# Attention scores with the key's low part against the query's high part alone, in half-height products

## The chip, the cores and the metric

The kernel runs on one core of one Trainium2 chip. The core's engines work side by side and each takes its own instructions in order: TensorE (PE in the profile; its weight loads are shown as PEld), VectorE (DVE), ScalarE (ACT), GpSimd (POOL), and SyncE (SP), which issues the transfers. The metric is the device time of one execution in microseconds.

## The reference

A block of three parts: attention with a bias that a small network makes of the distance of two positions, then a feed-forward layer with a ReLU6 gate, then one with a sigmoid gate.

```python
# attention: batch 4, heads 8, seq 576, head_dim 64
scores = scale * np.matmul(q, k.transpose(0, 1, 3, 2))
x = (psi_rel / psi_i)[..., None]
h = np.maximum(x @ w1 + b1, 0.0)
bias = h @ w2
scores = scores + bias.transpose(2, 0, 1)[None, :, :, :]
scores = scores - np.max(scores, axis=-1, keepdims=True)
attn = np.exp(scores)
attn = attn / (np.sum(attn, axis=-1, keepdims=True) + 1e-09)
y = np.matmul(attn, v)
# 2304 tokens of width 512; d_ff 2048, then 1536
h = x @ w_in;  z = (h * np.clip(h + 3.0, 0.0, 6.0) / 6.0) @ w_out
gate = 1.0 / (1.0 + np.exp(-(z @ w_gate)));  out = (gate * (z @ w_val)) @ w_out2
```

## The kernel before, in words

**Stages.** First the bias is computed and written to DRAM (products of L490). Then comes attention, and then the two feed-forward layers, whose products stand at L511 to L513, L575 and L632. The change touches attention alone, and the two calls of `prep` for the first unit, which stand in the bias stage.

**Units, steps and slots.** The 32 pairs of batch and head are taken two heads at a time: 16 units n, each with nine steps s. Steps 0 to 7 are one head h = s % 2 and one block of 128 queries c = s // 2. Step 8 has the last 64 queries of both heads. `slot_of_two` takes two steps at a time, so two units fill nine slots; in one of the nine the two steps are step 8 of a unit and step 0 of the next, and in another they are steps 7 and 8. A slot issues the scores of its own steps, then the products with the values (`av`) of older steps, then the exponentials, then the transposes of the probabilities of the slot before (`trans`, `trans_rem`), and last the preparation of a coming unit (`prep`). The framework's scheduler then orders each engine's instructions; the order that results is shown below.

**Scores.** Queries and keys are split in two parts of type fp32r: a high part, which is the rounded value, and a low part, the rest. The stationary operand `Q` has 128 rows: the 64 of the high part and, below them, the 64 of the low part. `K` holds the key's high part twice, one copy above the other, and the low part likewise, since the keys are loaded into both halves of the partitions. So one product of 128 rows with K's high part, and one with its low part, make a full product of both. With two halves of 288 keys (a = 0, 1) that is four products of 128 rows and 288 columns for a step, and eight for step 8 (L262). VectorE then adds the bias and takes the row's extreme in one instruction (L266); ScalarE exponentiates (L282).

**Around them.** The probabilities are transposed on TensorE: `tr` at L320, L335, L338 and L339 with 128 rows, L299 for the inverse sums, and L328 for step 8, in which a stationary operand has 64 rows, four products on the upper 64 rows of the array and four on the lower. `av` (L352) multiplies in fp32 with a stationary operand of 64 columns, one head on each half of the columns; L355 is its remainder with 128 columns. One `av` product leaves two records in the trace.

**Preparation.** `prep` makes the parts of one head: the query's high part on ScalarE (L230), the key's high part (L234), the query's low part and the key's low part (L238) on GpSimd. For unit 0 ScalarE and VectorE do it.

Of the kernel before, what the change touches and what calls it, by code (L numbers as in the profile page):

```python
# [10 lines left out]
F32 = mybir.dt.float32  # L11
F32R = mybir.dt.float32r
I32 = mybir.dt.int32
AF = mybir.ActivationFunctionType
ALU = mybir.AluOpType
# [3 lines left out]
P = 128  # L19
B, H, S, D = 4, 8, 576, 64  # L20
# [4 lines left out]
HS = S // 2  # L25
# [6 lines left out]
QH = (slice(0, S + 64), slice(S + 64, QW))  # L32
# [63 lines left out]
def block_kernel(ctx: ExitStack, tc: tile.TileContext, q, k, v, mlp, w_in, w_out, w_gate, w_val, w_out2, dist_d,  # L96
                 rows_d, out):
    nc = tc.nc
# [7 lines left out]
    one = keep.tile([P, 1], F32, name="one")  # L106
# [78 lines left out]
    apool = attn.enter_context(tc.tile_pool(name="apool", bufs=1))  # L185
    a2 = attn.enter_context(tc.tile_pool(name="a2", bufs=2))
# [3 lines left out]
    qn, kn, vn = {}, {}, {}  # L190
    cut = np.cumsum([0, QW, 2 * S, S // 2, 35, NPSI])
    q_in, k_in, bpsi, mlpc, rows = [early[:, i:j] for i, j in zip(cut, cut[1:])]
# [1 line left out]
    bias_t = [apool.tile([P, 2, S], F32, name=f"bias{c}") for c in range(4)]  # L194
    bias_m = apool.tile([P, S], F32, name="bias_m")
    Qs = [apool.tile([P, QW], F32R, name=f"q{i}") for i in range(2)]
    Ks = [apool.tile([P, 2, 2, S], F32R, name=f"k{i}") for i in range(2)]
    Pm = [apool.tile([P, S + 64], F32, name=f"pm{i}") for i in range(2)]
    ident = apool.tile([P, P], F32, name="ident")
    stat = apool.tile([P, 5, NSTEP], F32, name="stat")  # L200
# [4 lines left out]
    corr = apool.tile([P, 2], F32, name="corr")  # L205

    def load_qk(n):
        qn[n], kn[n] = q_in[0:D], k_in
        nc.sync.dma_start(qn[n], q[n])
        for r in range(2):  # L210
            nc.sync.dma_start(kn[n][D * r : D * r + D], k[n])

# [10 lines left out]

    def prep(n, h, on=PREP_ON):

        Q, K, qt, kt = Qs[n % 2][:, QH[h]], Ks[n % 2][:, :, h], qn[n][:, QH[h]], kn[n][:, h]

        def high(eng, out, x):
            if eng == "A":
                nc.scalar.copy(out, x)  # L230
            elif eng == "V":
                nc.vector.tensor_copy(out, x)
            else:
                nc.gpsimd.tensor_tensor(out=out, in0=x, in1=one[0 : x.shape[0]].to_broadcast(x.shape), op=ALU.mult)  # L234

        def low(eng, out, x, hi):
            eng = nc.vector if eng == "V" else nc.gpsimd
            eng.tensor_tensor(out=out, in0=x, in1=hi.bitcast(F32), op=ALU.subtract)  # L238

        high(on[0], Q[0:D], qt)  # L240
        high(on[1], K[:, 0], kt)
        low(on[2], Q[D:P], qt, Q[0:D])
        low(on[3], K[:, 1], kt, K[:, 0])

    halves = lambda ap: ap.rearrange("p (a b) -> p a b", a=2)
    NS = NU * NSTEP
# [3 lines left out]

    seq = [(n, s) for n in range(NU) for s in range(NSTEP)]

    def scores(t):
        n, s = seq[t]
        Q, K = Qs[n % 2], Ks[n % 2]
        ps = pp.tile([P, 2, 512], F32, name="s")
        todo = [(s % 2, s // 2)] if s < 8 else [(0, 4), (1, 4)]
        for a in range(2):
            mm = [(h, c, r) for h, c in todo for r in range(2)]
            for i, (h, c, r) in enumerate(mm):  # L260
                q0 = (0, S + P)[h] + P * c if c < 4 else (512, S)[h]
                last_s[0] = nc.tensor.matmul(ps[:, a, 0:HS], Q[:, q0 : q0 + P], K[:, r, h, HS * a : HS * a + HS],  # L262
                                 start=(i == 0), stop=(i == len(mm) - 1))
        u = a2.tile([P, S], F32, name="u", bufs=3)
        bt = bias_t[s // 2][:, s % 2] if s < 8 else bias_m
        last_u[0] = nc.vector.tensor_tensor_reduce(  # L266
            out=halves(u), in0=ps[:, :, 0:HS], in1=halves(bt), op0=ALU.add, op1=ALU.min, scale=-0.125, scalar=3e38,
            accum_out=low[n % 2][:, s : s + 1])
        us[t] = u

    def probs(t):
        n, s = seq[t]
# [94 lines left out]
    for n in range(NU):  # L367
        i = (NSTEP * n + 5) // 2 + 2
# [5 lines left out]
    def steps(i):  # L374
        return [t for t in (2 * i, 2 * i + 1) if 0 <= t < NS]

    def slot_of_two(i):

        for t in steps(i):
            scores(t)  # L380
            n, s = seq[t]
            p, b = divmod(n, B)
            if s == 0:
                last_v[0] = load_v(n)
            if b == B - 1 and p + 1 < NPAIR and (s % 2 == 1 or s == 8):
                load_bias(p + 1, s // 2)
        for n, a, g in AV.get(i, ()):
            av(n, a, g)
            if g == 4:
                av_out(n, a)  # L390
        for t in steps(i):
            expo(t)
        for t in steps(i - 1):
            n, s = seq[t]
            if s in (5, 8):
                invert(n, s // 6 * 3, s // 6 * 2 + 3)
        for t in steps(i - 2):
            n, s = seq[t]
            if s in (5, 8):
                turn_inv(n, s // 6 * 3, s // 6 * 2 + 3)  # L400
        for t in steps(i - 1):
            n, s = seq[t]
            with tc.issue_after(last_s[0].ins):
                trans(t)
                if s in REM:
                    trans_rem(n, REM[s])
        for t in steps(i):
            if t in PREP:
                n, h = PREP[t]
                prep(n, h)  # L410
            for k, (n, h) in PREP.items():
                if h == 1 and n + 1 < NU and t == k + 3:
                    load_qk(n + 1)
# [6 lines left out]
    with ExitStack():  # L420
# [18 lines left out]
            nc.tensor.matmul(ps, warm[:, 0:P], warm, start=True, stop=True)  # L439
        load_qk(0)  # L440
        make_identity(nc, ident)
        for i in range(2):
            nc.gpsimd.memset(Pm[i][:, 0:64], 0.0)

# [251 lines left out]
```

## Time and profile before

| what | value |
|---|---|
| three runs, device time | 1207.70, 1209.29, 1209.75 us (median 1209.29) |
| span of the profiled execution, from its first to its last instruction | 1205.7 us |
| median less span (start and end that the span leaves out) | 3.6 us |
| TensorE busy in the span | 1186.6 us (98%) |
| VectorE, ScalarE, GpSimd busy | 684.0, 573.8, 133.4 us |
| products of the scores (L262) | 640, 112.2 us of records at 310 ns |

Records of TensorE overlap, since the next product starts while the last one still drains; so 310 ns is how long one is under way, and not how far apart two of them are. What a product costs is read from the ends of neighbouring rows.

### The profile page before, as it was taken

The numbers are of one execution on the slowest core, as the hardware profiler recorded it, in microseconds if no ns is written. First come the engines' busy times: TensorE is split into PE (matmuls) and PEld (weight loads), VectorE is DVE, ScalarE is ACT, GpSimd is POOL, SyncE is SP. The second block draws the span as 40 slices with busy tenths as digits, with TensorE's granted clock in tenths as the row PEclk, the third lists the DMA queues.
The fourth block names the chain that finished last, engine by engine and source line by source line (L and its number), as shares of the span: only waits on it lengthen the run. The fifth ranks groups of instructions, "written<-read, shape, count | busy, mean of one in ns | idle before, by whom it ended". The sixth has DMA issues, their size and how long they took to land.

```text
span 1205.7 us, 18763 instructions
## 1 busy us (share of the span) xinstructions
PE 1186.6 (98%) x7302; PEld 1057.6 (88%) x7302; DVE 684.0 (57%) x1464; ACT 573.8 (48%) x1224; POOL 133.4 (11%) x108
## 2 busy tenths in 40 slices
PE   8999999999999999999999999999999999999998
PEld 3467777777789999999999999999999999999998
DVE  8977887778876555645565545654431544222332
ACT  7978877887854444434343434333321332221221
POOL 0055544554200000000000000000000000000000
PEclk9999999999999999999999999999999999999999
DMA  6644535453111232212222223322210121101000
GB/s 213 248 142 114 170 100 177 117 161 115 64 53 67 92 105 80 79 62 80 73 69 83 92 88 114 122 80 79 64 59 1 62 79 53 52 1 53 27 27 27
DMA packets 36152, 106.76 MB, mean 89 GB/s; under 512 B 3936, under 2 KB 10336, under 8 KB 36064
## 3 DMA queue, kind: packets, MB, share of 16 engines
q1 hardware_dynamic: 36064, 105.57, 26.9%
q8 instruction: 57, 0.93, 0.3%
q14 instruction: 31, 0.25, 0.1%
HBM read 80.78 MB, written 24.77 MB: 88 GB/s over the span
## 4 chain that ended last, share of the span: by engine, by line
PE 87%; DVE 6%; DMA 3%; ACT 3%; issue 1%; POOL 0%; SPq 0%; DVEq 0%; ACTq 0%; POOLq 0%
PE o L575 16%; PE h L513 13%; PE h L512 13%; PE h L511 13%; PE o L632 12%; PE s L262 5%; PE av L352 5%; PE tr L320 4%; PE s L490 3%; PE av L355 1%; DVE u L266 1%; DVE z L143 1%; DMA part<-raw 1%; DMA raw<-in_part_dram 1%; PE tr L299 1%
## 5 line engine op out<-in xcount | busy, mean ns | idle before, releaser
L511 PE MATMUL h<-early,slot 128*128 128x384 f32 x952 | 319.2, 335 | 0.0
L513 PE MATMUL h<-early,slot 128*128 128x384 f32 x952 | 319.2, 335 | 0.0
L512 PE MATMUL h<-early,slot 128*128 128x384 f32 x952 | 318.8, 335 | 0.0
L511 PEld LDWEIGHTS h<-early,slot 128*128 128x128 f32 x952 | 178.9, 188 | 2.6
L512 PEld LDWEIGHTS h<-early,slot 128*128 128x128 f32 x952 | 178.8, 188 | 2.5
L513 PEld LDWEIGHTS h<-early,slot 128*128 128x128 f32 x952 | 178.7, 188 | 0.1
L552 ACT CAST gh<-g 128x384 fp32r<-128x384 f32 x166 | 85.0, 513 | 162.3 <-DVE g L647 119.2
L575 PE MATMUL o<-gh,slot 128*128 128x384 f32 x768 | 157.0, 337 | 4.2 <-ACT raw L310 2.8
L647 DVE TENSOR_TENSOR g<-g,h 128x384 f32<-128x384 f32 x72 | 39.8, 553 | 182.2 <-PE h L513 182.2
L575 PEld LDWEIGHTS o<-gh,slot 128*128 128x128 f32 x768 | 134.2, 188 | 8.1 <-ACT raw L310 5.5
L553 DVE TENSOR_TENSOR gl<-g,gh 128x384 fp32r<-128x384 f32 x166 | 92.2, 558 | 78.8 <-ACT gh L552 76.8
L517 ACT ACTIVATE g<-h,half 128x384 f32<-128x384 f32 x94 | 54.5, 580 | 131.2 <-PE h L513 127.7
L262 PE MATMUL s<-k,q 128*128 128x288 f32 x640 | 112.2, 310 | 2.1 <-POOL k L238 1.0
L282 ACT ACTIVATE p<-u,stat 128x576 f32<-128x576 f32 x128 | 98.7, 773 | 32.3 <-DVE stat L266 31.9
L646 ACT ACTIVATE g<-h 128x384 f32<-128x384 f32 x72 | 35.4, 492 | 163.4 <-PE h L513 163.4
L632 PE MATMUL o<-slot,gh 128*128 128x512 f32 x432 | 111.9, 393 | 0.0
L266 DVE CUSTOM_DVE_ANT_0 u<-s,bias 128x576 f32<-128x576 f32 x128 | 93.4, 753 | 26.1 <-PE s L262 25.5
L518 DVE SCALAR_TENSOR_TENSOR g<-g,h 128x384 f32<-128x384 f32 x94 | 51.8, 552 | 95.5 <-ACT g L517 95.5
L262 PEld LDWEIGHTS s<-k,q 128*128 128x128 f32 x640 | 89.1, 189 | 5.4 <-POOL k L234 1.9
L632 PEld LDWEIGHTS o<-slot,gh 128*128 128x128 f32 x432 | 80.1, 188 | 13.5 <-issue 0.2
L575 PE MATMUL o<-gl,slot 128*128 128x384 f32 x384 | 88.5, 335 | 0.0
L352 PE MATMUL av<-ptm,vn 128*64 128x288 f32 x512 | 78.2, 419 | 1.2 <-DVE x L359 0.6
(99 smaller groups left out, 1495.8 us busy)
## 6 DMA issues: line engine op xcount, KB each, us to landing
raw<-in_part_dram SPq DMA_DIRECT2D x68, 512.0 KB, 3.6
nbias<-p SPq DMA_DIRECT2D x18, 576.0 KB, 3.2
early<-in_part_dram SPq DMA_DIRECT2D x32, 288.0 KB, 4.3
bias<-nbias SPq DMA_DIRECT2D x16, 576.0 KB, 6.4
take<-x SPq DMA_DIRECT2D x12, 768.0 KB, 4.2
vn<-in_part_dram SPq DMA_DIRECT2D x16, 320.0 KB, 3.2
early<-in_part_dram SPq DMA_DIRECT2D x16, 304.0 KB, 3.8
part<-raw SPq DMA_DIRECT2D x12, 384.0 KB, 2.7
```

The costliest lines, as they stand in the source:

```text
L262: last_s[0] = nc.tensor.matmul(ps[:, a, 0:HS], Q[:, q0 : q0 + P], K[:, r, h, HS * a : HS * a + HS], start=(i == 0), stop=(i == len(mm) - 1))
L266: last_u[0] = nc.vector.tensor_tensor_reduce(out=halves(u), in0=ps[:, :, 0:HS], in1=halves(bt), op0=ALU.add, op1=ALU.min, scale=-0.125, sc ...
L282: nc.scalar.activation(probs(t), us.pop(t), AF.Exp, bias=low[n % 2][:, s : s + 1], scale=-1.0, accum_out=sums[n % 3][:, s : s + 1])
L352: nc.tensor.matmul(ps[64 * h : 64 * h + 64, 0:HS], vt[:, 4 * h + g], ptm[:, h, g, cols], start=(g == 0), stop=False)
L511: nc.tensor.matmul(ps[:, 0:TW], wh, XH[:, c], start=(c == 0), stop=False)
L512: nc.tensor.matmul(ps[:, 0:TW], wl, XH[:, c], start=False, stop=False)
L513: nc.tensor.matmul(ps[:, 0:TW], wh, XL[:, c], start=False, stop=(c == 3))
L517: nc.scalar.activation(g, ph, AF.Relu, bias=half, scale=1.0 / 6.0)
L552: nc.scalar.copy(gh, g)
L553: last_g[0] = nc.vector.tensor_tensor(out=gl, in0=g, in1=gh.bitcast(F32), op=ALU.subtract)
L575: nc.tensor.matmul(os[c][:, 0:TW], sl[:, r, P * c : P * c + P], x, start=(first and r == 0 and x is gh), stop=(last and x is gl))
L632: nc.tensor.matmul(os[i], x[:, P * i : P * i + P], sl[:, r], start=(first and x is gh and r == 0), stop=(end and x is gl))
```

## The change

The key's low part no longer meets the query's low part. `K` holds the high parts of both heads and one low part (head 0 in the upper 64 partitions, head 1 in the lower). For head 1 the query's parts change places: high below, low above. For steps 0 to 7 each half of the keys gets one product of 128 rows (L272) and one of 64 rows, the query's high rows with the key's low rows (L281). The two steps of a slot are issued together: first the 128-row products of both, then the 64-row ones, the two steps' in turn; their heads lie on different halves of the rows. For step 8 a new operand `Qx` holds the high parts of the last 64 queries of both heads block-diagonally, and one product of 128 rows with both low parts (L275) makes three instead of four for each half of the keys. `prep` fills `Qx`, the key's low part is computed on 64 partitions instead of 128, and the queries are loaded by two transfers instead of one. The product of the two low parts is left out of the sum by this.

```diff
--- before.py
+++ after.py
@@ -194,7 +194,8 @@
     bias_t = [apool.tile([P, 2, S], F32, name=f"bias{c}") for c in range(4)]
     bias_m = apool.tile([P, S], F32, name="bias_m")
     Qs = [apool.tile([P, QW], F32R, name=f"q{i}") for i in range(2)]
-    Ks = [apool.tile([P, 2, 2, S], F32R, name=f"k{i}") for i in range(2)]
+    Ks = [apool.tile([P, 3, S], F32R, name=f"k{i}") for i in range(2)]
+    Qx = [apool.tile([P, P], F32R, name=f"qx{i}") for i in range(2)]
     Pm = [apool.tile([P, S + 64], F32, name=f"pm{i}") for i in range(2)]
     ident = apool.tile([P, P], F32, name="ident")
     stat = apool.tile([P, 5, NSTEP], F32, name="stat")
@@ -205,8 +206,9 @@
     corr = apool.tile([P, 2], F32, name="corr")
 
     def load_qk(n):
-        qn[n], kn[n] = q_in[0:D], k_in
-        nc.sync.dma_start(qn[n], q[n])
+        qn[n], kn[n] = q_in, k_in
+        for r in range(2):
+            nc.sync.dma_start(qn[n][D * r : D * r + D, QH[r]], q[n][:, QH[r]])
         for r in range(2):
             nc.sync.dma_start(kn[n][D * r : D * r + D], k[n])
 
@@ -223,24 +225,27 @@
 
     def prep(n, h, on=PREP_ON):
 
-        Q, K, qt, kt = Qs[n % 2][:, QH[h]], Ks[n % 2][:, :, h], qn[n][:, QH[h]], kn[n][:, h]
-
-        def high(eng, out, x):
+        own, other = (slice(0, D), slice(D, P))[:: 1 - 2 * h]
+        Q, K, qt, kt = Qs[n % 2][:, QH[h]], Ks[n % 2], qn[n][own, QH[h]], kn[n]
+        c4 = (slice(512, S), slice(S + 64, S + P))[h]
+
+        def high(eng, out, x, rows=slice(0, P)):
             if eng == "A":
                 nc.scalar.copy(out, x)
             elif eng == "V":
                 nc.vector.tensor_copy(out, x)
             else:
-                nc.gpsimd.tensor_tensor(out=out, in0=x, in1=one[0 : x.shape[0]].to_broadcast(x.shape), op=ALU.mult)
+                nc.gpsimd.tensor_tensor(out=out, in0=x, in1=one[rows].to_broadcast(x.shape), op=ALU.mult)
 
         def low(eng, out, x, hi):
             eng = nc.vector if eng == "V" else nc.gpsimd
             eng.tensor_tensor(out=out, in0=x, in1=hi.bitcast(F32), op=ALU.subtract)
 
-        high(on[0], Q[0:D], qt)
-        high(on[1], K[:, 0], kt)
-        low(on[2], Q[D:P], qt, Q[0:D])
-        low(on[3], K[:, 1], kt, K[:, 0])
+        high(on[0], Q[own], qt)
+        high(on[1], K[:, h], kt[:, h])
+        low(on[2], Q[other], qt, Q[own])
+        low(on[3], K[own, 2], kt[own, h], K[own, h])
+        high(on[1], Qx[n % 2][own, D * h : D * h + D], qn[n][own, c4], own)
 
     halves = lambda ap: ap.rearrange("p (a b) -> p a b", a=2)
     NS = NU * NSTEP
@@ -250,23 +255,39 @@
 
     seq = [(n, s) for n in range(NU) for s in range(NSTEP)]
 
-    def scores(t):
-        n, s = seq[t]
-        Q, K = Qs[n % 2], Ks[n % 2]
-        ps = pp.tile([P, 2, 512], F32, name="s")
-        todo = [(s % 2, s // 2)] if s < 8 else [(0, 4), (1, 4)]
+    def q_cols(h, c):
+        q0 = (0, S + P)[h] + P * c if c < 4 else (512, S)[h]
+        return slice(q0, q0 + P)
+
+    def scores(ts):
+
+        pss = [pp.tile([P, 2, 512], F32, name="s") for _ in ts]
+        ks = [slice(HS * a, HS * a + HS) for a in range(2)]
+        for t, ps in zip(ts, pss):
+            n, s = seq[t]
+            Q, K = Qs[n % 2], Ks[n % 2]
+            for a in range(2):
+                todo = [(s % 2, s // 2)] if s < 8 else [(0, 4), (1, 4)]
+                for i, (h, c) in enumerate(todo):
+                    last_s[0] = nc.tensor.matmul(ps[:, a, 0:HS], Q[:, q_cols(h, c)], K[:, h, ks[a]],
+                                                 start=(i == 0), stop=False)
+                if s == 8:
+                    last_s[0] = nc.tensor.matmul(ps[:, a, 0:HS], Qx[n % 2], K[:, 2, ks[a]], start=False, stop=True)
         for a in range(2):
-            mm = [(h, c, r) for h, c in todo for r in range(2)]
-            for i, (h, c, r) in enumerate(mm):
-                q0 = (0, S + P)[h] + P * c if c < 4 else (512, S)[h]
-                last_s[0] = nc.tensor.matmul(ps[:, a, 0:HS], Q[:, q0 : q0 + P], K[:, r, h, HS * a : HS * a + HS],
-                                 start=(i == 0), stop=(i == len(mm) - 1))
-        u = a2.tile([P, S], F32, name="u", bufs=3)
-        bt = bias_t[s // 2][:, s % 2] if s < 8 else bias_m
-        last_u[0] = nc.vector.tensor_tensor_reduce(
-            out=halves(u), in0=ps[:, :, 0:HS], in1=halves(bt), op0=ALU.add, op1=ALU.min, scale=-0.125, scalar=3e38,
-            accum_out=low[n % 2][:, s : s + 1])
-        us[t] = u
+            for t, ps in zip(ts, pss):
+                n, s = seq[t]
+                if s < 8:
+                    r = slice(D * (s % 2), D * (s % 2) + D)
+                    last_s[0] = nc.tensor.matmul(ps[:, a, 0:HS], Qs[n % 2][r, q_cols(s % 2, s // 2)],
+                                                 Ks[n % 2][r, 2, ks[a]], start=False, stop=True)
+        for t, ps in zip(ts, pss):
+            n, s = seq[t]
+            u = a2.tile([P, S], F32, name="u", bufs=3)
+            bt = bias_t[s // 2][:, s % 2] if s < 8 else bias_m
+            last_u[0] = nc.vector.tensor_tensor_reduce(
+                out=halves(u), in0=ps[:, :, 0:HS], in1=halves(bt), op0=ALU.add, op1=ALU.min, scale=-0.125, scalar=3e38,
+                accum_out=low[n % 2][:, s : s + 1])
+            us[t] = u
 
     def probs(t):
         n, s = seq[t]
@@ -376,8 +397,8 @@
 
     def slot_of_two(i):
 
+        scores(steps(i))
         for t in steps(i):
-            scores(t)
             n, s = seq[t]
             p, b = divmod(n, B)
             if s == 0:
@@ -439,6 +460,8 @@
             nc.tensor.matmul(ps, warm[:, 0:P], warm, start=True, stop=True)
         load_qk(0)
         make_identity(nc, ident)
+        for i in range(2):
+            nc.gpsimd.memset(Qx[i].bitcast(F32), 0.0)
         for i in range(2):
             nc.gpsimd.memset(Pm[i][:, 0:64], 0.0)
 
```

TensorE's order in a slot whose two steps both have 64-row products. Here `s` are the scores, `tr` transposes, `av` products with the values; k_110 and q_108 are the buffers of every second unit. Before:

```order
L352 MATMUL av<-ptm,vn 64x288 x6
L320 MATMUL tr<-ident,p 128x128 x8
L335 MATMUL tr<-ident,p 128x128
L262 MATMUL s<-k_110,q_108 128x288 x8
L352 MATMUL av<-ptm,vn 64x288 x2
L355 MATMUL av<-ptr,vn 128x288
```

TensorE's order at the same place now; L341, L356, L373 and L376 are what L320, L335, L352 and L355 were:

```order
L373 MATMUL av<-ptm,vn 64x288 x6
L341 MATMUL tr<-ident,p 128x128 x8
L356 MATMUL tr<-ident,p 128x128
L272 MATMUL s<-k_110,q_108 128x288 x4
L281 MATMUL s<-k_110,q_108 128x288 x4
L373 MATMUL av<-ptm,vn 64x288 x2
L376 MATMUL av<-ptr,vn 128x288
```

Eight products of 128 rows have become four of 128 rows and a run of four of 64 rows, two on each half of the rows.

TensorE's order in the first slot of a unit, before (L299 transposes the inverse sums):

```order
L262 MATMUL s<-k_110,q_108 128x288 x8
L352 MATMUL av<-ptm,vn 64x288 x6
L299 MATMUL tr<-ident,spread 128x128 x3
L320 MATMUL tr<-ident,p 128x128 x4
L328 MATMUL tr<-ident,pm_113 128x64 x4
```

TensorE's order at the same place now:

```order
L272 MATMUL s<-k_110,q_108 128x288 x2
L281 MATMUL s<-k_110,q_108 128x288 x2
L373 MATMUL av<-ptm,vn 64x288
L272 MATMUL s<-k_110,q_108 128x288 x2
L281 MATMUL s<-k_110,q_108 128x288 x2
L373 MATMUL av<-ptm,vn 64x288 x5
L320 MATMUL tr<-ident,spread 128x128 x3
```

The 64-row products stand in two runs, each with one head alone, and one `av` product has come to stand between them, away from the other five.

TensorE's order in the slot of step 8 and the next unit's step 0, before (k_111 and q_109 are that unit's buffers):

```order
L262 MATMUL s<-k_110,q_108 128x288 x8
L262 MATMUL s<-k_111,q_109 128x288 x4
L352 MATMUL av<-ptm,vn 64x288 x6
```

TensorE's order at the same place now:

```order
L272 MATMUL s<-k_110,q_108 128x288 x2
L275 MATMUL s<-k_110,qx_112 128x288
L272 MATMUL s<-k_110,q_108 128x288 x2
L275 MATMUL s<-k_110,qx_112 128x288
L272 MATMUL s<-k_111,q_109 128x288 x2
L281 MATMUL s<-k_111,q_109 128x288 x2
L373 MATMUL av<-ptm,vn 64x288 x6
```

Step 8 has six products instead of eight, all of 128 rows, and the two 64-row products of step 0 have no partner on the other half of the rows.

## Rows read from the trace of the kernel before

**Rows 1.** The page: span, and TensorE's busy time, its share and instructions.

```profile
span 1205.7 us, 18763 instructions
PE 1186.6 (98%) x7302; PEld 1057.6 (88%) x7302; DVE 684.0 (57%) x1464; ACT 573.8 (48%) x1224; POOL 133.4 (11%) x108
```

**Rows 2.** Busy time by stretch: attention, then the rest; PEclk is the granted clock.

```profile
core 0: us, PE busy (x) PEld busy (x) DVE busy (x) ACT busy (x) POOL busy (x), PEclk, DMA share, GB/s
60.20:340.00 279.80, 273.50 (x2010) 208.64 (x2010) 220.70 (x555) 223.46 (x582) 132.50 (x100) 1.00 0.42 125
```

**Rows 3.** The chain that ended last, 60 to 340 us, shares by line.

```profile
by line: PE s L262 23.5%; PE av L352 19.2%; PE tr L320 16.9%; PE av L355 5.9%; DVE u L266 3.7%; DMA raw<-in_part_dram 3.0%; PE tr L299 2.8%; DVE z L143 2.6%; PE tr L328 2.3%; PE tr L335 2.2%; DVE ptm L312 2.0%; DVE z L134 1.9%; DMA early<-i
```

**Rows 4.** Timeline of TensorE, a slot of two steps: start us, duration us, group.

```profile
174.21 0.27 PE L335 MATMUL tr<-ident,p 128*128 128x128 f32 x1
174.24 1.30 PE L262 MATMUL s<-k,q 128*128 128x288 f32 x8
175.47 0.71 PE L352 MATMUL av<-ptm,vn 128*64 128x288 f32 x4
176.10 0.75 PE L355 MATMUL av<-ptr,vn 128*128 128x288 f32 x2
```

**Rows 5.** Timeline of TensorE at another place, from 162.5 us.

```profile
162.25 0.83 PE L262 MATMUL s<-k,q 128*128 128x288 f32 x5
163.01 1.68 PE L352 MATMUL av<-ptm,vn 128*64 128x288 f32 x12
164.62 0.55 PE L299 MATMUL tr<-ident,spread 128*128 128x128 f32 x3
165.00 0.60 PE L320 MATMUL tr<-ident,p 128*128 128x128 f32 x4
165.53 0.46 PE L328 MATMUL tr<-ident,pm 64*128 64x64 f32 x4
165.92 0.80 PE L262 MATMUL s<-k,q 128*128 128x288 f32 x4
...
167.40 0.27 PE L338 MATMUL tr<-ident,pm 128*128 128x128 f32 x1
167.51 0.27 PE L339 MATMUL tr<-ident,pm 128*64 128x128 f32 x1
```

**Rows 6.** Timeline of TensorE: both heads' 64-row transposes in one run.

```profile
80.00 0.47 PE L328 MATMUL tr<-ident,pm 64*128 64x64 f32 x8
```

**Rows 7.** Weight loads in attention by line and shape: count, busy, mean ns, idle before.

```profile
L262 PEld LDWEIGHTS s<-k,q 128*128 128x128 f32 x640 | 89.1, 189 | 5.4 <-POOL k L234 1.9 <-POOL k L238 1.2 <-DVE stat L266 0.8
L320 PEld LDWEIGHTS tr<-ident,p 128*128 128x128 f32 x512 | 58.7, 141 | 9.8 <-ACT inv L310 3.5 <-DVE ptm L312 1.3 <-DVE z L141 1.3
L352 PEld LDWEIGHTS av<-ptm,vn 128*64 128x64 f32 x496 | 30.8, 136 | 23.9 <-issue 9.5 <-DVE x L359 1.3 <-DVE ptm L312 0.8
L355 PEld LDWEIGHTS av<-ptr,vn 128*128 128x128 f32 x60 | 8.9, 188 | 13.1 <-issue 13.1
L328 PEld LDWEIGHTS tr<-ident,pm 64*128 64x128 f32 x128 | 7.7, 138 | 5.6 <-issue 1.7 <-ACT p L282 1.5 <-ACT spread L293 1.2
```

**Rows 8.** Waits in attention, longest first: total us, times, longest us.

```profile
POOL k L234 <- PE s L262: 37.9, 11, 8.2
DVE u L266 <- PE s L262: 32.8, 34, 3.0
```

**Rows 9.** Groups in attention that bound the costs off TensorE, and the reduction.

```profile
L266 DVE CUSTOM_DVE_ANT_0 u<-s,bias 128x576 f32<-128x576 f32 x128 | 93.4, 753 | 26.1 <-PE s L262 25.5
L238 POOL TENSOR_TENSOR k<-early,k 128x576 fp32r<-128x576 f32 x30 | 42.3, 1421 | 0.5
L234 POOL TENSOR_TENSOR k<-early,one 128x576 fp32r<-128x576 f32 x30 | 33.8, 1147 | 56.6 <-PE s L262 37.9 <-DMA early<-in_part_dram 18.7
L310 ACT COPY ptr<-tr 64x64 f32<-64x64 f32 x16 | 3.2, 203 | 3.6 <-PE tr L339 3.4
```

## The prediction

> **What bounds the kernel now.** I read the page first: TensorE is busy for 98% of a span of 1205.7 us [rows 1]. Since its records overlap, that proves little, so I looked at attention alone. There (60.2 to 340 us) TensorE has 273.5 of 279.8 us, ScalarE 223, VectorE 221, GpSimd 133, and the granted clock is 1.00, the 2.4 GHz level [rows 2]. The chain of that stretch runs through TensorE's lines: 23.5% scores, 19.2% and 5.9% `av`, 16.9% and some 7% transposes; the largest term of another engine is VectorE's 3.7% [rows 3]. So attention is bound by how long TensorE's instructions take one after another, and the change must be priced there.
>
> **What one instruction costs.** Ends of neighbouring rows give it. The eight scores end at 174.24 + 1.30 = 175.54, the transpose ahead of them at 174.48: 1.06 / 8 = 0.1325 us each [rows 4]. A pair of `av` products on the two halves of the columns leaves four records; the run of three pairs ends 163.01 + 1.68 - 163.08 = 1.61 us after the scores ahead of it, the run of one pair 176.18 - 175.54 = 0.64 us after [rows 4, 5]. Two pairs more cost 0.97, one pair 0.485 us, and each run has 0.155 us that belongs to no product.
>
> That remainder stands wherever the shape of the stationary operand changes between 128 rows by 128 columns and half of it. `av` to L299: 165.17 - 164.69 = 0.48 us for three transposes; four of L320 behind them take 0.43, so 0.108 each, and 0.15 is left. L320 to L328 (64 rows): 0.39 us for four transposes of 64 columns, at half of 0.108 each 0.17 too much. L328 to four scores: 166.72 - 165.99 = 0.73, less 0.53, is 0.20 [rows 5]. `av` to L355: 0.67 for half a pair's columns twice over, less 0.485, is 0.19 [rows 4]. Between one full shape and another there is none (L335 to scores, L299 to L320). The price follows the weight load that comes next: 136 ns for `av`, 141 for transposes, 138 for L328, but 188 and 189 for L355 and the scores [rows 7]. It looks as if the engine empties and the next load, otherwise hidden, stands bare, with some 10 ns more.
>
> The Trainium skill states such a rule, in TensorEngine Tiling (Array Packing), Key Properties: a change of tiling mode, not of the tile, drains TensorE. It gives no duration, so by the rule alone the sign of this change stays open. The trace agrees for L352 and L328, and not for L339, whose 128x64 transpose ends 0.11 us after L338 like any other [rows 5]; the rows decide. The same page, Theoretical Speedup, puts contractions of 64 rows at up to 2x. By that without any drain, the 256 64-row products would cost 128 steps of 0.1325 and the change would give 21 us.
>
> **The change, part by part.** I went down TensorE's whole order of both programs and counted; the pieces shown are typical.
>
> *Products.* Of 640 scores 352 with 128 rows remain (320 of L272, 32 of L275): 288 x 0.1325 = 38.2 us less. L281 adds 256 of 64 rows and 288 columns. Two heads' 64-row products can run side by side: eight of L328, four on each half of the rows, take 0.47 us where four take 0.46 [rows 5, 6]. I take a pair for one step of 0.1325. If all in slots of two were paired there would be 144 steps; but 16 of the 72 slots hold step 8 and leave their other step alone, and the order cuts other slots into runs with one head (first slot of a unit, above). In each run the longer side counts: 175 steps in 97 runs, 23.2 us. The order also pulls `av` runs apart (one product, then five): 141 pair times in place of 130, 11 x 0.485 = 5.3 us more, and L328 likewise 0.2. Sum of products: -38.2 + 23.2 + 5.3 + 0.2 = -9.5 us.
>
> *Changes of shape.* Before there are 177: 66 into `av` (0.15), 23 into L328 (0.17), 40 into transposes from a half shape (0.15), 32 into L355 (0.19), 16 into scores (0.20): 29.1 us. Afterwards there are 319: 94 into L281, 77 into `av`, 21 into L328 (then L349), 73 into transposes, 32 into L376, 22 into 128-row scores. L281's entry the trace does not show. Its load has 64 rows like L328's and 128 columns of scores like L262's. Rows do not set a load's time (138 ns for 64, 141 for 128), the kind does, so I take 189 ns and 0.20 us; the lower end is 0.15. That makes 55.4 us, 26.3 more. Where `av` follows at once the exit costs nothing new, since `av` had its entry before; where transposes follow it is paid in full.
>
> *Other engines.* GpSimd gets two copies of 64x64 a unit (at most 1.15 us, the time of 128x576) and its low part of the key costs the same with half the partitions [rows 9]. It has 147 us free [rows 2] and works a unit ahead, so nothing. In the bias stage ScalarE gets two copies of 64x64 at 0.20 us [rows 9]: 0 to 0.4 us, taken as 0. One more transfer for the queries of a unit, of the same bytes in sum: nothing, a unit ahead as well; for unit 1, which starts late, some tenths. The reductions (0.75 us each [rows 9]) now both wait for the last 64-row product of a slot; before, the first ran during the second step's scores. VectorE already waits 32.8 us for scores [rows 8]. Behind it stand the copies that free the transposes' PSUM, and ScalarE's exponentials. From the slot's scores to the next slot's lie at least one `av` pair, L355 and nine transposes, 0.64 + 0.67 + 0.97 = 2.3 us, against two reductions (1.5 us) and one copy. I take 0; the end is some 6 us (below).
>
> **Sum:** -9.5 + 26.3 = +16.8 us on the profiled execution: a span of 1222.5 us. The median lies 3.6 us above the span; the prediction is 1226 us. The feed-forward layers (350 us to the end) keep their products and only start later.
>
> **The rivals.**
> *A, faster: half height without a bare load.* If L281 keeps the 128-row shape's mode, its entries and exits are free. Then the order has 196 changes worth 32.1 us, 3.0 more than before, and the sum is -9.5 + 3.0 = -6.5: 1203 us. For it speaks L339, which changes shape and pays nothing [rows 5]; against it, that L328, with the same 64 rows, pays 0.17 on entry and 0.20 on exit even where a run uses one half of the rows alone [rows 5]. With the exits as priced it decides once an entry costs under 0.2 - 16.8 / 94 = 0.02 us. 8%. The speed-up that the Trainium skill allows (TensorEngine Tiling (Array Packing), Theoretical Speedup) is A with every 64-row product paired: 1188 us. The order's runs with one head speak against it; 1% of the 8.
>
> *B, no pairs.* If 64-row products of 288 columns run one after another, 256 x 0.1325 = 33.9 us in place of 23.2: 1237 us. The pairs of L328 speak against it [rows 6], though their moving operand is only 64 columns wide and of another type. 6%.
>
> *C, the late reductions come back to TensorE.* Where another 0.7 to 1.8 us of VectorE's work stands ahead of the reductions, the 2.3 us are used up, and the next scores (two PSUM buffers) or the transposes of late probabilities wait. At 0.1 us in 56 slots with pairs it is 6 us: 1232. ScalarE and VectorE have a fifth of the stretch free [rows 2], which speaks for a smaller sum. 12%.
>
> *D, the gaps swallow it.* TensorE's waits in attention, 279.8 - 273.5 = 6.3 us and a little hidden in records, could shrink while it is the slower one: at most 6 us less, 1220. 8%; with the entry at 0.15 us as well (4.7 us less) 1215. Within 0.2% (2.4 us, about what a measurement of this kernel tells from no change) of 1209.3 it would only be with free entries and paid exits: 16.8 - 94 x 0.20 = -2.0, so 1207; 4%.
>
> **How the numbers follow.** The forecast of 1226 with its bounds (lower entry price 1221, small waits 1230) has 62%. To leave out no more than 2 in 10 the range takes in D and C and the lower part between: 1212 to 1235; A lies below it and B's full price above. Slower by over 0.2% are the forecast, B, C and D, 88%; same 4%; faster, A, 8%.
>
> **What the profile will show.** Right: the rows of L281 come in runs whose ends lie 0.20 us later than the products explain, with idle time of the weight loads ahead of them put down to "issue"; four L281 of two heads end in about 0.47 us after the 128-row scores (0.20 and two steps); single `av` products stand alone; the records of scores fall by 32 in count, attention ends some 17 us later, and the stretch from there to the end is unchanged. Wrong: entries to L281 at 0.13 us after the last score (A); pairs 0.13 us apart (B); waits of scores or transposes for VectorE or ScalarE that grow by microseconds (C). The step most likely to fail is the entry price, since no row of before has a 64-row product of fp32r.

## The result, and the profile after

The changed kernel takes 1218.14 us (median of 4 runs, 1217.4 to 1218.4), and the kernel before takes 1208.74 us (4 runs, 1207.7 to 1209.75). The ratio is 1.0084, with a 95% interval of 1.0072 to 1.0096 (the two medians give 1.0078): 0.8% slower. The forecast was 1226 us with a range of 1212 to 1235. Sign and range held; the loss is 9.4 us where the prediction's sum has 16.8.

The page of the changed kernel, span and busy time (as [rows 1]):

```profile
span 1215.6 us, 18800 instructions
PE 1200.9 (99%) x7270; PEld 1048.0 (86%) x7270; DVE 672.8 (55%) x1464; ACT 575.9 (47%) x1226; POOL 142.1 (12%) x140
```

TensorE has 32 instructions fewer and 14.3 us more of busy time. The chain of 60 to 340 us by line (as [rows 3]) shows where: the scores' two lines hold 25.2% of it, where one line of 640 products held 23.5%.

```profile
by line: PE av L373 20.4%; PE tr L341 17.1%; PE s L272 13.1%; PE s L281 12.1%; PE av L376 5.8%; issue 5.3%; PE tr L320 3.1%; PE tr L356 2.9%; POOL k L242 2.5%; POOL k L238 2.4%; PE tr L349 2.4%; DVE z L141 1.6%; DMA early<-in_part_dram 1.6%
```

The timeline of TensorE in the changed kernel (start, duration, group; as [rows 4]): first a slot with a pair, then the slot of step 8.

```profile
179.16 0.27 PE L356 MATMUL tr<-ident,p 128*128 128x128 f32 x1
179.19 0.76 PE L272 MATMUL s<-k,q 128*128 128x288 f32 x4
179.88 0.53 PE L281 MATMUL s<-k,q 64*128 64x288 f32 x4
180.34 0.71 PE L373 MATMUL av<-ptm,vn 128*64 128x288 f32 x4
180.98 0.75 PE L376 MATMUL av<-ptr,vn 128*128 128x288 f32 x2
...
183.34 0.42 PE L272 MATMUL s<-k,q 128*128 128x288 f32 x2
183.69 0.53 PE L281 MATMUL s<-k,q 64*128 64x288 f32 x2
```

Read the ends. The 128-row scores end at 179.95, the four 64-row ones at 180.41: 0.46 us. Two of L281 without a partner take as long, 184.22 - 183.76 = 0.46 us. So two run side by side, a step is 0.1325 us as before, and 0.46 - 0.265 = 0.195 us is the change of shape. `av` behind them ends 0.64 us later, just as it did behind 128-row scores [rows 4]. In this slot eight products of 1.06 us [rows 4] have become 0.52 + 0.46 = 0.98 us: each pair saves one step of 0.1325 us, so the slot's two pairs save 0.265 us, and they pay 0.195.

Weight loads in attention of the changed kernel (as [rows 7]):

```profile
L272 PEld LDWEIGHTS s<-k,q 128*128 128x128 f32 x320 | 47.3, 189 | 8.4 <-issue 3.3 <-DVE stat L287 2.4 <-POOL k L238 0.9
L373 PEld LDWEIGHTS av<-ptm,vn 128*64 128x64 f32 x494 | 32.5, 136 | 24.3 <-issue 9.9 <-ACT ptr L331 0.7 <-DMA vn<-in_part_dram 0.5
L281 PEld LDWEIGHTS s<-k,q 64*128 64x128 f32 x256 | 27.1, 184 | 16.0 <-issue 13.8 <-POOL k L242 1.0 <-POOL qx L238 0.2
```

A 64-row load of the scores takes 184 ns, a 128-row one 189: the number of rows hardly matters. Ahead of L281 the loads stood idle for 13.8 us put down to "issue", with no engine that they waited for.

**Where the 9.9 us of span come from.** I took TensorE's records in attention in order and gave each the spacing found above (scores 0.1325, transposes 0.109 or 0.062, `av` 0.242 a record, of which two run side by side) and each change of shape its price (into L281 0.194, `av` 0.147, L328 0.143, transposes 0.150, L355 and scores 0.198). Where an end lies over 30 ns later than that, the excess counts as waiting. "After attention" is the time from attention's last record to TensorE's last one; 3.7 us of the span follow behind it in every run. The same was done for every run below:

```
kernel                 changes   us  waits  attention  after attention   span   against before
before                    179   28.8  10.2    288.5        853.3        1205.7
changed                   321   54.5   6.5    300.5        850.7        1215.6   1.0084
full rows                 200   32.1   7.7    290.7        850.7        1205.9   1.0002
twice the changes         473   83.8   5.9    328.8        850.2        1243.5   1.0339
full rows, in turn        195   31.3  11.5    291.1        850.5        1205.7   1.0008
whole runs                245   41.3  24.8    296.4        850.2        1210.9   1.0063
singles full              288   48.6  11.8    297.5        851.1        1212.6   1.0055
values whole              264   44.1  15.8    297.6        851.3        1213.4   1.0057
values whole, full        186   29.7  15.7    293.4        851.2        1209.2   1.0010
no low part               226   35.9  12.8    273.0        849.5        1187.3   0.9818
full, free start          192   30.8  10.4    290.1        850.7        1205.3   0.9987
pairs, free start         275   46.1   9.5    294.8        850.2        1209.5   1.0038
full, slot's order        184   29.6  19.6    295.1        850.7        1209.6   1.0040
```

(Two changes in each row belong to feed-forward products that already stand in attention.) Where the granted clock is at its 1.2 GHz level ends come later too, and that is counted as waiting: such stretches hold 9.5 us of the waits of "values whole, full", 8.8 of "whole runs", 5.3 of "values whole", 4.8 of "singles full", 3.9 of "no low part" and 3.2 of "full, free start", and none in "before" and "changed". From before to changed: changes +25.7, waits -3.7, products -10.0 (what is left of attention's +12.0), the bias stage +0.5, the stretch after attention -2.6.

### The profile page after: what moved, and what is told of

Same layout as the page of the kernel before. It is cut to its first block, busy times and chain, and to the rows that moved or that the text cites. A ratio compares the mean times of both kernels' runs of the same rounds, so it can differ in the third digit from the quotient of the medians.

```text
span 1215.6 us, 18800 instructions
## 1 busy us (share of the span) xinstructions
PE 1200.9 (99%) x7270; PEld 1048.0 (86%) x7270; DVE 672.8 (55%) x1464; ACT 575.9 (47%) x1226; POOL 142.1 (12%) x140
## 4 chain that ended last, share of the span: by engine, by line
PE 90%; DVE 3%; ACT 2%; issue 2%; POOL 2%; DMA 1%; SPq 0%; DVEq 0%; POOLq 0%; ACTq 0%
PE o L598 16%; PE h L536 13%; PE h L534 13%; PE h L535 13%; PE o L655 12%; PE av L373 5%; PE tr L341 4%; PE s L272 3%; PE s L281 3%; PE s L513 3%; PE av L376 2%; PE tr L320 1%; PE tr L356 1%; PE tr L349 1%; POOL k L242 1%
## 5 line engine op out<-in xcount | busy, mean ns | idle before, releaser
L575 ACT CAST gh<-g 128x384 fp32r<-128x384 f32 x166 | 85.0, 512 | 162.4 <-DVE g L670 119.8
L373 PE MATMUL av<-ptm,vn 128*64 128x288 f32 x512 | 85.6, 420 | 0.0
L341 PE MATMUL tr<-ident,p 128*128 128x128 f32 x512 | 72.7, 276 | 1.1 <-ACT inv L331 1.1
L272 PE MATMUL s<-k,q 128*128 128x288 f32 x320 | 70.1, 322 | 1.3 <-DVE stat L287 1.2
```

The lines of the kernel that those rows point to most:

```text
L272: last_s[0] = nc.tensor.matmul(ps[:, a, 0:HS], Q[:, q_cols(h, c)], K[:, h, ks[a]], start=(i == 0), stop=False)
L341: nc.tensor.transpose(ps[:, kc], pts[n, c][:, h, 64 * h + P * kc : 64 * h + P * kc + P], ident)
L373: nc.tensor.matmul(ps[64 * h : 64 * h + 64, 0:HS], vt[:, 4 * h + g], ptm[:, h, g, cols], start=(g == 0), stop=False)
L575: nc.scalar.copy(gh, g)
```

## The experiments

Three runs were made for the price of a change of shape, the others for what is left when it is paid less often. In all runs that use 128 rows for a low product the query's low part also meets the other head's low part.

**Full rows.** One line of the changed kernel:

```diff
-                    r = slice(D * (s % 2), D * (s % 2) + D)
+                    r = slice(0, P)
```

> One line differs from the changed kernel: the low-part product of steps 0 to 7 uses all 128 rows (query high and low rows against both heads' low parts), so the sum also takes in a product of the query's low part with the other head's low part; the product count is the same, 608, and nothing runs side by side. Theory (changes of the array's shape decide): the 94 entries at 0.194 us go, and the exits behind them; counted in the new order, with the spacings of the traces, 198 changes and 31.8 us in place of 319 and 54.2, products 245.7 us in place of 234.5, together 11.2 us less than the changed kernel, of which waits may take back up to 5: 1207 to 1212 us. Rival (the joint order of two steps and its late reductions cost the time): the joint order is still there, so 1216 us or more.

Measured: 1207.12 us, ratio 1.0002 (0.9993 to 1.0010). The same number of products, none of them side by side, and 0.8% less than the changed kernel by the two ratios (9.7 us of span, 9.8 us of attention). The joint order of two steps and its late reductions are still in it, so they are not what costs. Pairing is the loss, by its changes of shape.

**Twice the changes.** The loop over the two halves of the keys is put outside:

```diff
-        for t, ps in zip(ts, pss):
-            ...
-            for a in range(2):
+        for a in range(2):
+            for t, ps in zip(ts, pss):
+                ...
...
-        for a in range(2):
```

> The changed kernel with the loop over the two halves of the keys outside: per half first the 128-row products of both steps, then the 64-row ones. Same products, but 166 entries to the 64-row shape in place of 94 and 471 changes in place of 319. Theory of the changes: 29 us more than the changed kernel by the spacings of its trace, waits give back up to 5: 1242 to 1248 us. Rival (a change is hidden behind waits that are there anyway): under 1230 us.

Measured: 1247.79 us (four runs, 1243.7 to 1251.2), ratio 1.0339 (1.0310 to 1.0367). The timeline of TensorE:

```profile
178.25 0.40 PE L280 MATMUL s<-k,q 64*128 64x288 f32 x1
178.57 0.40 PE L272 MATMUL s<-k,q 128*128 128x288 f32 x1
178.90 0.39 PE L280 MATMUL s<-k,q 64*128 64x288 f32 x1
```

Each product that follows one of the other shape ends 0.32 us after it, 0.13 for itself and 0.19 for the change. 152 changes more cost 29.3 us of price and 27.9 us of span: they are not hidden.

**No low part.** The 64-row products are left out.

```diff
-                                                 start=(i == 0), stop=False)
+                                                 start=(i == 0), stop=(s < 8))
...
-                if s < 8:
+                if s < 8 and t < 0:
```

> The changed kernel without the key's low part in steps 0 to 7: the 256 64-row products are left out, their operands are still prepared. By the order 224 changes, 35.6 us, products 219.3 us: 254.9 us, 33.8 less than the changed kernel. If TensorE's sum sets the time alone, 1184 us; with waits that grow as TensorE gets faster, up to 1197 us. Rival (other engines hold the stage, so the sum of TensorE is not what the change moved): 1205 us or more.

Measured: 1186.58 us, ratio 0.9818 (0.9801 to 0.9836). The page's windows of attention in this run:

```profile
61.00:334.00 273.00, 267.55 (x1770) 183.60 (x1770) 216.37 (x565) 226.38 (x589) 142.96 (x130) 0.99 0.43 129
```

TensorE is busy for 267.6 of 273 us even now; ScalarE has 226 and VectorE 216. Attention is 27.5 us shorter than in the changed kernel: the stage follows TensorE's sum in the main, and the waits, which grow from 6.5 to 12.8 us, take 6.3 us of the 33.8 back.

**Full rows, in turn.** As full rows, but each step's scores are issued for themselves:

```diff
-        scores(steps(i))
         for t in steps(i):
+            scores([t])
```

> As the kernel with the 128-row low product (the same additional product), but the scores of a slot's two steps are issued one step after another, as before the change. Products 608 as well; by the order 193 changes, 30.9 us, products 243.5 us: 3.1 us less than with the joint order and 2.0 us more than before. Theory of the changes: 1206 to 1212 us, about 3 us under the run with the joint order. Rival (late reductions): 6 us or more under it.

Measured: 1207.58 us, ratio 1.0008 (0.9999 to 1.0016). The time lies in the theory's range, but not 3 us under the run with the joint order, nor 6 us, as the rival had it: it is the same within the intervals. The sum is 3.1 us smaller than with the joint order, but the waits are 3.8 us longer (11.5 against 7.7). This is close to the part of the change that only shortens step 8: 32 products, 4.2 us, are saved, 16 changes of shape come with the new order, and nothing is left.

**Singles full, and values whole.** The 64-row products without a partner use 128 rows, and `av` is queued behind its slot's scores:

```diff
-                    r = slice(D * (s % 2), D * (s % 2) + D)
+                    r = slice(D * (s % 2), D * (s % 2) + D) if len(ts) == 2 and all(seq[x][1] < 8 for x in ts) else slice(0, P)
...
-            av(n, a, g)
+            with tc.issue_after(last_s[0].ins):
+                av(n, a, g)
```

> The changed kernel with two things: 64-row products without a partner use 128 rows (with the product of the query's low part and the other head's low part added there), and the products with the values are queued behind their slot's last score. By the order 286 changes of shape, 48.3 us, products 232.1 us: 280.4 us, 8.3 less than the changed kernel, 8.0 more than before. Theory of the changes: 1208 to 1213 us, between the kernel before and the changed one. Rival (waits set the time, not TensorE's sum): no nearer to before than 1217 us.

Measured: 1215.46 us, ratio 1.0055 (1.0042 to 1.0067): 2.5 us above what the theory gave and 1.5 under the rival. 33 changes less than the changed kernel are worth 5.9 us of price, and 5.3 us of waits came back.

**Whole runs, and values whole.** TensorE is chained in the order in which the slot is written: 64-row products behind all 128-row ones, `av` behind them, transposes behind `av`, and (in whole runs alone) the next slot's scores behind the transposes:

```diff
+        with tc.issue_after(last_pe[0].ins) if last_pe[0] is not None else ExitStack():
+            scores(steps(i))
...
+            with tc.issue_after(last_pe[0].ins):
+                av(n, a, g)
...
-            with tc.issue_after(last_s[0].ins):
+            with tc.issue_after(last_pe[0].ins):
                 trans(t)
```

> The changed kernel with TensorE kept in the order in which a slot is written: all 128-row products, then all 64-row ones, then the products with the values, then transposes, then the next slot; where a slot has no partner for a 64-row product, that one uses 128 rows (with the product of the query's low part and the other head's low part added there). By the order 243 changes, 41.0 us, products 224.6 us: 265.6 us, which is 23 less than the changed kernel and 7 less than before. Theory of the changes: 1195 to 1206 us if the stiff order brings few waits. Rival (waits of a stiff order for VectorE and ScalarE, or late reductions): 1209 us or more, with waits of scores or transposes that grow by over 5 us.

> As the run with whole runs, but the next slot's scores may mix with the transposes of this one; 64-row products still stand behind all 128-row ones of their slot and the products with the values behind them (and the low product of a slot without a partner uses 128 rows, with the product of the low parts of both heads added). By the order 262 changes, 43.8 us, products 231.2 us: 275.0 us, 9 more than with whole runs. Theory (the sum plus waits that a stiff order adds): the 24.8 us of waits in the run with whole runs fall to about 8, so 1203 to 1211 us. Rival (the joint order of the scores makes the waits): they stay above 18 us, 1214 us or more.

> As the run before it, but every low product of steps 0 to 7 uses 128 rows (with the product of the low parts of both heads added), so nothing of the scores changes the shape. By the order 184 changes, 29.4 us, products 242.8 us: 272.2 us, 2.8 less than with paired 64-row products. Theory of the changes: 1200 to 1208 us, 0 to 4 us under the run with pairs in the same order. Rival (pairs pay once their runs are whole): 2 us or more above it.

Measured: whole runs 1214.47 us, ratio 1.0063 (1.0046 to 1.0079); values whole 1215.41, 1.0057 (1.0044 to 1.0069); with full rows 1209.62, 1.0010 (1.0000 to 1.0019). The smaller sums are there, but the waits have grown to 24.8, 15.8 and 15.7 us, so all three lie above what the theory gave, and whole runs are where the rival put them. The rival of values whole has its time, but not the waits above 18 us that it gave as the reason; with full rows the time is 5.8 us less than with pairs, so pairs do not pay here either. In the run with whole runs part of them come back in every two units. TensorE's timeline there (idle before in brackets):

```profile
125.41 0.60 PE L343 MATMUL tr<-ident,p 128*128 128x128 f32 x4
125.85 0.27 PE L358 MATMUL tr<-ident,p 128*128 128x128 f32 x1
126.69 0.66 PE L343 MATMUL tr<-ident,p 128*128 128x128 f32 x4 [0.57 <-ACT ptm L333]
```

Transposes that come one behind another wait for ScalarE to empty their PSUM. In the two others most of the waits stand in one place, the start of unit 1; the values whole with full rows, timeline and windows there (columns of the windows as in [rows 2]):

```profile
75.16 0.85 PE L272 MATMUL s<-k,q 128*128 128x288 f32 x2 [2.94 <-POOL k L238]
76.27 0.85 PE L272 MATMUL s<-k,q 128*128 128x288 f32 x2 [0.26 <-POOL k L238]
79.09 0.85 PE L281 MATMUL s<-k,q 128*128 128x288 f32 x2 [1.97 <-POOL k L242]
79.87 3.15 PE L373 MATMUL av<-ptm,vn 128*64 128x288 f32 x12
```

```profile
70.00:75.00 5.00, 2.22 (x16) 1.62 (x14) 2.63 (x9) 4.95 (x15) 2.74 (x3) 1.00 0.78 182
75.00:80.00 5.00, 2.61 (x8) 1.64 (x10) 1.35 (x3) 1.83 (x5) 4.85 (x5) 0.51 0.22 57
80.00:85.00 5.00, 5.00 (x22) 3.17 (x23) 1.00 (x3) 1.35 (x3) 4.58 (x6) 0.50 0.46 125
85.00:90.00 5.00, 5.00 (x40) 3.74 (x38) 3.35 (x9) 2.85 (x8) 3.09 (x3) 0.96 0.33 89
```

GpSimd prepares unit 1 late; in a stiff order the products that could fill the gap are queued behind its scores. TensorE stands still for 2.9 us, the granted clock falls to the 1.2 GHz level, and the run of twelve `av` records takes 3.15 us, where it takes 1.68 at the 2.4 GHz level ([rows 5], and in this run from 90 us on).

**A free start.** The first eight slots keep the scheduler's order (`if i >= 8` at each chain, or `if ts[0] >= 16`, which is the same slot); then full rows, pairs, and full rows with the whole slot chained:

> As the run with the values whole and every low product on 128 rows (which adds the product of the low parts of both heads), but the first eight slots keep the scheduler's own order. By the order 190 changes, 30.4 us, products 243.8 us: 274.2 us, 2.0 more than with the stiff start. In that run's profile the start, 75 to 85 us, has waits of 3.4 and 2.4 us for GpSimd's preparation of unit 1 and 10.2 us at the lower clock. Theory (the stiff start and the clock behind it cost some 10 us of the 15.7 us of waits): clock 1.00 throughout, waits 5 to 7 us, 1200 to 1205 us. Rival (these waits would only come later in the order): 1207 us or more.

> The same freedom for the run with the values whole and paired 64-row products (the slot without a partner on 128 rows, with the product of the low parts of both heads added). By the order 273 changes, 45.7 us, products 232.7 us: 278.5 us, 4.3 more than with 128 rows in the same order. Theory of the changes: 1204 to 1211 us, 2 to 6 us over the run with 128 rows. Rival (pairs pay, what hid it was the start): under the run with 128 rows.

> As the run with whole runs, with every low product on 128 rows and the first eight slots in the scheduler's own order. By the order 182 changes, 29.3 us, products 240.9 us: 270.2 us, the smallest sum of all with the low part. The run with whole runs had 1.7 us of waits in every two units (transposes for their PSUM, scores for the reduction), 14 us in all, which stay if the slot's order makes them: 1202 to 1208 us. If they go with the start: 1193 to 1200 us.

Measured: full rows 1205.82 us, ratio 0.9987 (0.9979 to 0.9996), 3.8 us less than with the stiff start; pairs 1211.86, 1.0038 (1.0026 to 1.0050); the slot's order 1212.37, 1.0040 (1.0028 to 1.0052). All three lie above what the theory gave, by 0.8, 0.9 and 4.4 us or more. The start costs less, but not nothing. TensorE's windows of full rows with the free start:

```profile
75.00:80.00 5.00, 3.41 (x15) 2.11 (x16) 0.43 (x2) 1.69 (x5) 4.70 (x6) 0.87 0.23 62
80.00:85.00 5.00, 5.00 (x32) 3.95 (x31) 3.32 (x9) 3.23 (x8) 4.85 (x5) 0.79 0.43 119
```

The clock still dips there, to 0.87 and 0.79, where 1.00 was expected, and the waits are 10.4 us instead of 5 to 7. In almost the same order (with pairs the 64-row products are chained as well) pairs are 6.0 us slower than full rows (4.7 us in attention); the sum of the order said 4.3. Chaining the whole slot has the smallest sum and 19.6 us of waits, of which 13.5 lie behind 90 us, where full rows without that chain have 3.1: the waits are made by the slot's order and not by the start. Full rows with a free start is the only one with the low part that lies below the kernel before, by 0.13%, which is within the 0.2% that the prediction set as hardly to be told from no change.

## Why the prediction was right, and where its size was off

**What bounds the stage.** Right: leaving out products moves the time mostly by their sum (no low part: 33.8 us less of products and changes, 27.5 us less of attention).

**Products, -9.5 us.** Measured -10.0, as the remainder. Pairs do run side by side, in steps of 0.1325 us; rival B is out. The single `av` products that the new order leaves, 5.3 us of the sum, are in the trace too: 18 runs there hold one product alone, and 4 before.

**Changes of shape, +26.3 us.** Measured +25.7. The entry into L281, which no row of before showed, is 0.194 us; the value was taken from the load's kind (189 ns) and not from its rows, and the load came out at 184 ns. With that rival A is out, and the run with full rows shows the same from the other side. The rule of the Trainium skill (TensorEngine Tiling (Array Packing), Key Properties: changing the tiling mode drains the engine) gives no duration; the trace agrees for L281, with 0.194 us as the price. Whether the 128x64 transpose of L339 changes the mode at all no row tells, so that it pays nothing does not decide against the rule. The Trainium skill's speed-up for contractions of 64 rows (TensorEngine Tiling (Array Packing), Theoretical Speedup, up to 2x) is there too: a pair takes one step of 0.1325 us instead of two. But a run of two pairs, one for each half of the keys, saves 0.265 us, which is too little to pay the entry of 0.194 and a full exit of 0.15 or 0.20.

**Waits, taken as 0.** This is the step that failed in size. TensorE's waits in attention fell from 10.2 to 6.5 us. (The prediction had read 6.3 us and a little more from the busy time; by the ends it was 10.2.) The waits of transposes behind scores went from 5.1 us to 0.5 behind 128-row scores and 1.3 behind 64-row ones. That is the size of rival D, given 8%, but mostly not its reason, that TensorE is the slower one. Full rows and full rows in turn differ in one place, the joint order of a slot's two steps, and their attention is about equally long (290.7 and 291.1 us); yet these waits are 1.8 us with the joint order and 7.8 in turn. From 60 to 362 us the run in turn has two waits of transposes for VectorE and ScalarE (total us, times, longest us) that the run with the joint order does not have:

```profile
PE tr L341 <- DVE ptm L333: 2.1, 3, 0.7
PE tr L341 <- ACT inv L331: 1.4, 3, 0.5
```

So the joint order, whose late reductions the prediction feared and took at 0, takes 3.8 us of waits away. Longer slots take little: from full rows to the changed kernel attention grows by 9.8 us and the waits fall by 1.2; with twice the changes it grows by 28.3 us more and they fall by 0.6. These figures come from one profiled execution of each kernel. With the fewer waits attention ends 12.5 us later (361.2 against 348.7 us), where some 17 were forecast. Rival C did not happen: with the same joint order and no pairs the time is that of before.

**The feed-forward layers only start later.** They took 2.6 us less in the profile, 850.7 against 853.3 us, and 849.5 to 851.3 in all eleven experiments, with and without pairs. TensorE's waits for PSUM there are 4.1 us in the profile of before (L575 for ScalarE and VectorE) and 2.2 in the changed one. TensorE takes its feed-forward products in the same order in both; in the trace of before a product ends over 0.6 us after the one ahead of it at four places (391, 460, 596 and 664 us), in those of the changed kernel and of every experiment at two. The profile of before is one execution, and its runs spread by 5 us (1205.2 to 1210.0), so it may be that execution alone; its span of 1205.7 us, which is about the median of 21 other executions (1205.3), speaks rather against that. This stays open.

**The 3.6 us between span and median.** One execution's span was set against the median of several executions. In the changed kernel the difference is 2.5 us (1.8 that the span leaves out, and 0.7 by which the profiled execution was faster than the median), so 1.1 us of the 7.9 us by which the forecast missed lies there. The rest is in the table: waits 3.7, the stretch after attention 2.6, products and changes 1.1, less 0.5 for the later start.

## What to carry to other kernels

Before products are packed on half of the array's rows, count in the built order how often the shape will change, price each change by the bare weight load that follows (here 0.14 to 0.20 us), and set that against what one run of packed products saves (here 0.1325 us a pair, so an entry with a full exit takes about three pairs): a run has to be several pairs long, or end where a change was due anyway. Price the order too, since moved products can pull other packed runs apart (here `av`, 5 us by the count). And look at the waits in the new order, which here went both ways: issuing two steps jointly took 3.8 us of them away, while orders made for TensorE's sum alone brought some 3 to 18 us.

## What the runs showed of the hardware

Products on different halves of the rows go side by side even when they are of different kinds and lengths. In the changed kernel 64-row transposes start and end between the 64-row scores:

```profile
171.39 0.40 PE L281 MATMUL s<-k,q 64*128 64x288 f32 x2
171.64 0.21 PE L349 MATMUL tr<-ident,pm 64*128 64x64 f32 x1
171.64 0.39 PE L281 MATMUL s<-k,q 64*128 64x288 f32 x1
171.69 0.35 PE L349 MATMUL tr<-ident,pm 64*128 64x64 f32 x3
171.85 0.37 PE L281 MATMUL s<-k,q 64*128 64x288 f32 x1
```

The two scores beside them end 0.24 and 0.19 us after the score before (171.79, 172.03, 172.22), so it is not free, since a step is 0.1325 us; but no entry of its own stands ahead of the transposes.

In the run with the values whole and full rows a wait of 2.9 us in attention was followed by the lower clock, the 1.2 GHz level, over 75 to 85 us (0.51 and 0.50), although TensorE worked without a pause in the second half of that time.
